# Identity products moved ahead of a conditioning step on TensorE, in a hand-ordered block of attention and a gated mixer

## The chip, the cores and the metric

The kernel runs on one core of one Trainium2 chip. The metric is device time in microseconds (us) of one execution, as the median of several. An execution is a little longer than the span of the instructions in its profile. Each core has TensorE (PE, matrix products), VectorE (DVE), ScalarE (ACT), GpSimd (POOL) and SyncE (SP, which here only issues transfers); they run on their own and wait for one another by semaphores.

## What is computed

The reference is a transformer block whose two branches are modulated by a conditioning vector c. All data are bf16, x has 2048 rows of 448.

```python
mod = (silu(c) @ w_mod).reshape(1, 6, 1, -1)          # sa, ca, ga, sb, cb, gb
h = layernorm(x) * (1 + ca) + sa
x = x + ga * A(h)      # 16 heads of 28, causal, window 256: softmax(q k^T) v, then wo
h = layernorm(x) * (1 + cb) + sb
x = x + gb * B(h)      # z = gelu(h w_in); z1 * (w_sp @ layernorm(z2) + b_sp), then w_out
```

What matters here is the beginning: sa and ca must be known, two pairs of x tiles (128 rows each) must be normalised, transposed and modulated, and only then can the first q and k be projected.

## The kernel before, in words

The whole program is a list of numbered operations, each made by a helper with its dependencies, and one hand-kept text, ORDER (lines 19 to 145), that says in which order each engine takes them. A word such as `57.p.2` means: operation 57 goes to TensorE (p; a is ACT, v is DVE, g is POOL, s is SP) and takes option 2 of what it has to hold, here a PSUM bank. `order` reads the words, `count` and `waits` work out the semaphores, and `emit` writes each engine's stream. An engine takes its stream strictly in that order, so an operation that waits holds up all that stand behind it on the same engine. A TensorE operation that only follows another TensorE operation into the same bank needs no semaphore.

The head of the program, up to about 20 us, works in these steps, each named by the line that the profile shows:

- Operation 46 (L518) turns the row c into a column; ScalarE takes the SiLU (L522, L523).
- Operations 54, 55 and 56 (created at L546, products at L540 with one at L544) form sa and ca from three pieces of w_mod: nine, sixteen and eight products with one column each. Each of the three waits for its own piece of wmod to land. VectorE copies the result to modT (L552, L553).
- Tiles 0 and 1 of x go through statistics (L605 to L617) and a norm (L625 on DVE, L627 on ACT). Operations 165 and 162 (L692) transpose them on TensorE, four products of 128 columns each; DVE (L701) and ACT (L699) apply sa and ca on the way into hT.
- WQK, the padded q and k weights, is copied together from wq_st by DVE and ACT (L596) and POOL (L597).
- Operations 174 to 183 (L740) project q for those 256 rows, first by slices of the contraction (174 and 175 use slice 0, 176 and 177 slice 1, 178 and 179 slice 2, two products each), then the last slice for each group; 188 to 191 begin k. qT and KT are copied out by L767 and L768.
- Tiles 2 and 3 follow the same path: statistics on DVE, the power on POOL (L613), the norms, then the transposes 168 and 171, the remaining projections, the exponentials (L913) on ScalarE, and attention proper.

Between these stand identity products, created by `warm` at lines 558 to 566 as operations 57 to 110: one product of the 128 x 128 identity with itself repeated over 512 columns (L561). Their result is never read. Of the 54, ORDER names those that are used, and the others are dropped. Each takes a PSUM bank from the list bA, whose options 0 to 7 are banks 6, 7, 0, 1, 2, 3, 4, 5. After the head the kernel runs attention tile by tile, then the gated mixer's first products (L1081, L1127), then the spatial mixing (L1151) and the output (L1170).

Of the kernel before, what the change touches and what calls it, by code (L numbers as in the profile page):

```python
# [17 lines left out]

ORDER = """
2.a 25.v 35.g 0.s 26.v 27.v 28.v 38.g 39.g 3.a 4.s 36.g 45.a 33.g 29.v 5.s 30.v 31.v 37.g 32.v 40.g 6.s 7.s 41.g 46.p.0 48.a 47.a 144.v 8.s 145.v 1.s  # L20
138.v 146.g 57.p.2 58.p.3 59.p.4 60.p.5 61.p.6 62.p.7 54.p.1 9.s 147.g 139.v 140.v 10.s 141.g 148.v 55.p 149.a.0 34.g 11.s 142.v 56.p 143.v.1 132.g
14.s 71.p.0 72.p.3 165.p.2 112.v 111.v 162.p.3 12.s 131.v 130.a 166.v 133.g 163.v 16.s 167.a 73.p.6 74.p.7 75.p.0 76.p.6 174.p.4.5 150.v 164.a 13.s
175.p.6.7 50.a 77.p.0 176.p 151.v 15.s 156.v 177.p 152.g 178.p 153.g 179.p 135.a 157.v 183.p 181.p 158.v 134.v 180.p 159.g 154.v 187.a 188.p.0.1 185.v
189.p.2.3 155.a.2 136.g 190.p 160.v 191.p 161.v.3 42.g 168.p.7 171.p.5 137.g 192.p 169.v 193.p 49.g 194.p 172.v 182.p 170.a 197.p 195.p 196.p 173.v
198.a 43.g 234.v 199.a 204.p.7 51.g 184.a 232.v 203.p.5 200.a 186.a 205.p.0 235.v 201.a 236.v 52.g 207.a 202.p.1 208.a 230.v 382.p.0 209.a 224.p.6
206.a 231.v 237.v 383.a.0 233.v 219.s 238.v 239.g 210.p.7 221.s 225.v 222.p.0 220.s 44.g 240.v 213.p.1 244.v.0 218.s 241.v.1 223.a 242.v.2 388.p.0
# [1228 lines left out]
```

## Time and profile before

| what | value |
|---|---|
| median of 3 runs | 273.93 us (273.01 to 274.91) |
| profiled execution | 275.39 us, span 273.7 us |
| TensorE busy | 266.2 us of the span |
| identity products (L561) | 13 in the span: 6, then 2, 4 and 1 |
| VectorE, ScalarE, POOL busy | 155.6, 137.9, 106.2 us |

A row of the profile's timeline gives the start and the length in us, the engine, the line of the kernel, the operation, the tile written and the tiles read, the shape, and the count of merged instructions; in brackets stands how long the engine was idle before and what ended that. A row of the chain of waits gives the start, the length and what the end of the program was waiting for then. Products on TensorE overlap, so the length of a merged row is the spacing times the count less one, and the duration of the last.

### The profile page before, as it was taken

To read this page: it belongs to the slowest core of one execution; us is meant where nothing else is said; L and a number is where in the kernel's file an instruction comes from. 1 tells how busy PE (TensorE), PEld (TensorE's weight loads), DVE (VectorE), ACT (ScalarE), POOL (GpSimd) and SP (SyncE) were. 2 spreads that over 40 slices of the span, in tenths; PEclk is the share of its full clock that TensorE was granted. 3 is DMA by queue.
4 is the path that set the end of the run, shared out by engine and by line. 5 is a ranking of instruction groups with operands and counts; after the bars stand their busy time and mean duration, and the time that the engine had idled before them with its cause. 6 is when DMAs were issued, how large, how long until landed. Compare 5 with 4: busy or idle time off the path is not lost.

```text
span 273.7 us, 7480 instructions
## 1 busy us (share of the span) xinstructions
PE 266.2 (97%) x3232; PEld 143.0 (52%) x3232; DVE 155.6 (57%) x380; ACT 137.9 (50%) x190; POOL 106.2 (39%) x161
## 2 busy tenths in 40 slices
PE   5989999999999999999999999999999999999995
PEld 2665565566578665545444444444444444444543
DVE  6689998799998999998483001131102321136533
ACT  3579999999999999799997400000000000000000
POOL 7650507401225715663458600646003631156220
PEclk9999999999999999999999999999999999999999
DMA  7938734633036755645999999500000000001212
GB/s 217 308 149 258 230 82 101 92 70 38 17 74 111 109 98 104 146 103 99 188 174 190 182 188 194 82 0 0 0 2 0 0 0 2 0 0 40 88 59 84
DMA packets 67594, 26.53 MB, mean 97 GB/s; under 512 B 58021, under 2 KB 66474, under 8 KB 67562
## 3 DMA queue, kind: packets, MB, share of 16 engines
q1 hardware_dynamic: 67288, 25.61, 45.4%
q8 instruction: 25, 0.41, 0.6%
q10 hardware_dynamic: 274, 0.46, 0.5%
q14 instruction: 7, 0.06, 0.1%
HBM read 9.53 MB, written 1.84 MB: 42 GB/s over the span
## 4 chain that ended last, share of the span: by engine, by line
PE 89%; ACT 7%; DMA 2%; DVE 1%; issue 1%; SPq 0%; DVEq 0%
PE ps L1151 35%; PE ps L1081 8%; PE ps L1127 8%; PE ps L1170 8%; PE ps L782 6%; PE ps L995 6%; PE ps L952 4%; ACT PW L913 4%; PE ps L1019 4%; PE ps L824 3%; PE ps L961 2%; DMA wmod<-in_w_mod_dram 2%; PE ps L811 1%; PE ps L561 1%; PE ps L740 1%; ACT qT L767 1%
## 5 line engine op out<-in xcount | busy, mean ns | idle before, releaser
L913 ACT ACTIVATE PW<-ps 128x2048 bf16<-128x2048 f32 (+1 forms) x56 | 67.9, 1255 | 1.8 <-PE ps L952 0.7
L1155 DVE TENSOR_TENSOR tmpg<-ps,bsp_bc 128x512 bf16<-128x512 f32 x28 | 19.0, 689 | 85.6 <-PE ps L1151 74.0
L1158 POOL TENSOR_TENSOR z1T<-tmpg,z1T 128x512 bf16<-128x512 bf16 x28 | 31.9, 1151 | 75.3 <-DVE tmpg L1155 75.3
L1151 PE MATMUL ps<-wspB,z 128*128 128x512 bf16 x224 | 49.5, 379 | 0.0
L1151 PE MATMUL ps<-wspA,z 128*128 128x512 bf16 x224 | 49.0, 379 | 0.0
L968 DVE TENSOR_TENSOR PT<-PW,mask 128x1024 bf16<-128x1024 bf16 x56 | 36.6, 681 | 0.7 <-ACT PW L913 0.7
L1151 PEld LDWEIGHTS ps<-wspA,z 128*128 128x128 bf16 x224 | 21.9, 98 | 26.7 <-POOL z L1096 0.5
L1151 PEld LDWEIGHTS ps<-wspB,z 128*128 128x128 bf16 x224 | 21.9, 98 | 26.3
L613 POOL TENSOR_TENSOR rs_all<-ve_all,neghalf 128x1 f32<-128x1 f32 (+1 forms) x31 | 20.6, 674 | 35.1 <-DVE ve_all L610 33.8
L995 PE MATMUL ps<-Vaug,PT 128*128 128x32 bf16 x496 | 23.9, 177 | 0.0
L995 PEld LDWEIGHTS ps<-Vaug,PT 128*128 128x128 bf16 x496 | 21.9, 96 | 3.8 <-DVE o_sb L1011 0.6
L1170 PE MATMUL ps<-w_out_g,z1T 128*128 128x448 bf16 (+2 forms) x126 | 21.9, 332 | 0.0
L1081 PE MATMUL ps<-w_in,hT 64*128 64x448 bf16 x224 | 21.9, 349 | 0.0
L1127 PE MATMUL ps<-hT,w_in 64*128 64x512 bf16 x196 | 21.8, 376 | 0.0
L995 PE MATMUL ps<-Vaug,PW 128*128 128x32 bf16 x224 | 20.2, 176 | 0.0
L782 PE MATMUL ps<-hT,WQK 128*128 128x512 bf16 x80 | 20.1, 380 | 0.0
L605 DVE BATCH_NORM_STATS2 st_all<-x_sb 128x6 f32<-128x448 bf16 x32 | 18.9, 610 | 0.0
L995 PEld LDWEIGHTS ps<-Vaug,PW 128*128 128x128 bf16 x224 | 17.6, 96 | 2.2
L1170 PEld LDWEIGHTS ps<-w_out_g,z1T 128*128 128x128 bf16 x126 | 11.7, 98 | 10.0
L1135 ACT ACTIVATE z1T<-ps 128x512 bf16<-128x512 f32 x28 | 14.3, 609 | 4.5 <-PE ps L1127 4.5
L1081 PEld LDWEIGHTS ps<-w_in,hT 64*128 64x128 bf16 x224 | 10.7, 94 | 10.6 <-ACT PW L913 0.4
L952 PE MATMUL ps<-qT,KT 32*128 32x64 bf16 (+2 forms) x1008 | 15.3, 198 | 0.3 <-ACT PW L913 0.2
(122 smaller groups left out, 343.5 us busy)
## 6 DMA issues: line engine op xcount, KB each, us to landing
out_dram<-fin SPq DMA_DIRECT2D x15, 112.0 KB, 1.7
x_sb<-in_A_x_dram SPq DMA_DIRECT2D x3, 448.0 KB, 4.2
wmod<-in_w_mod_dram SPq DMA_DIRECT2D x1, 1344.0 KB, 8.2
w_in<-in_B_w_in_dram SPq DMA_DIRECT2D x1, 1344.0 KB, 9.5
QBD<-qT SPq DMA_DIRECT2D x16, 64.0 KB, 2.1
w_out_g<-in_B_w_out_dram SPq DMA_DIRECT2D x1, 784.0 KB, 6.3
bsp_bc<-in_B_b_sp_dram SPq DMA_DIRECT2D x1, 512.0 KB, 5.4
x_sb<-in_A_x_dram SPq DMA_DIRECT2D x2, 224.0 KB, 3.7
```

Source lines behind the costliest of these rows:

```text
L613: rs = pool(0.41 + 0.155 * len(tiles), lambda e: e.tensor_tensor(rs_all[:, slot, a:b], ve_all[:, slot, a:b], neghalf[:, 0:b - a], ALU.pow) ...
L782: m = pe(4 * MMS, [lambda e, h=h, g=g, kc=kc, tb=tb: e.matmul(ps[:, h.slot[0], :], lhsT=WQK[:, kc, 4 * g:4 * g + 4, :].rearrange("p a b -> ...
L913: ex = act(xdur, lambda e, out_ap=out_ap, in_ap=in_ap: e.activation(out_ap(), in_ap(), ACT.Exp, scale=SCALE), [s], v - 8.0 + u, takes, tab ...
L952: fm.append(lambda e, hm=hm, k=k, qi=qi, key=key, kn=kn, lo=lo, hi=hi, col=col, p0=p0, t=t, j=j: e.matmul(ps[p0:p0 + kn, hm.slot[t], k * 1 ...
L968: return dve(0.68, lambda e: e.tensor_tensor(cols(hp.slot[0] * 2048 + 1024 * k, [[256, 4], [128, 2], [1, 128]]), cols(at_w() + 128 + 192 * ...
L995: fns.append(lambda e, hp=hp, hO=hO, hi=hi, bi=bi, kb=kb, hd=hd, nb=nb, a=at[hi][bi], p_of=p_of: e.matmul(ps[:, hO.slot[0], 32 * hd:32 * h ...
L1081: return lambda e, kc, p0, start, stop: e.matmul(ps[:, hs[t % 2].slot[hf], 0:D], lhsT=hT[p0:p0 + 64, kc, t * 128:(t + 1) * 128], rhs=w_in[ ...
L1127: return lambda e, kc, p0, start, stop: e.matmul(ps[:, hs[b // 2].slot[b % 2], :], lhsT=w_in[p0:p0 + 64, kc, ft * 128:(ft + 1) * 128], rhs ...
L1151: m = pe(16 * MMS, [lambda e, h=h, si=si, ft=ft, tb=tb: e.matmul(ps[:, h.slot[0], :], lhsT=z2[:, si, ft * 128:(ft + 1) * 128], rhs=(wspA i ...
L1155: a = dve(0.7, lambda e, h=h, ht=ht, tb=tb: e.tensor_tensor(tmpg[:, ht.slot[0], :], ps[:, h.slot[0], :], bsp_bc[:, tb * 512:(tb + 1) * 512 ...
L1158: u = pool(1.16, lambda e, ht=ht, ft=ft, tb=tb: e.tensor_tensor(z1T[tb][:, ft, :], tmpg[:, ht.slot[0], :], z1T[tb][:, ft, :], ALU.mult), [ ...
L1170: return [lambda e, ft=ft: e.matmul(ps[:, h.slot[0], c0:c1], lhsT=z1T[t // 4][:, ft, (t % 4) * 128:(t % 4 + 1) * 128], rhs=w_out_g[:, ft, ...
```

## The change

ORDER alone is changed; no operation is made differently. On TensorE the identity products are placed anew. The numbers 57, 58 and so on only count them off; all are the same product.

| place in TensorE's order | before | after |
|---|---|---|
| between 46 (c) and 54 (first L540 products) | 6 | 9 |
| between 56 (last L540 products) and 165 (first transposes) | 2 | 0 |
| between 162 (transposes) and 174 (first q products) | 4 | 3 |
| between 175 and 176 (q, slices 0 and 1) | 1 | 0 |
| in all | 13 | 12 |

The three that are added in front write banks 0, 1 and 2, which the first three have written; the three behind the transposes write banks 6, 4 and 5. Every other word stands in the same order on its engine; the rest of the changed lines is where the text breaks.

```diff
-138.v 146.g 57.p.2 58.p.3 59.p.4 60.p.5 61.p.6 62.p.7 54.p.1 9.s 147.g 139.v 140.v 10.s 141.g 148.v 55.p 149.a.0 34.g 11.s 142.v 56.p 143.v.1 132.g
-14.s 71.p.0 72.p.3 165.p.2 112.v 111.v 162.p.3 12.s 131.v 130.a 166.v 133.g 163.v 16.s 167.a 73.p.6 74.p.7 75.p.0 76.p.6 174.p.4.5 150.v 164.a 13.s
-175.p.6.7 50.a 77.p.0 176.p 151.v 15.s 156.v 177.p 152.g 178.p 153.g 179.p 135.a 157.v 183.p 181.p 158.v 134.v 180.p 159.g 154.v 187.a 188.p.0.1 185.v
+138.v 146.g 57.p.2 58.p.3 59.p.4 60.p.5 61.p.6 62.p.7 63.p.2 64.p.3 65.p.4 54.p.1 9.s 147.g 139.v 140.v 10.s 141.g 148.v 55.p 149.a.0 34.g 11.s 142.v
+56.p 143.v.1 132.g 14.s 165.p.2 112.v 111.v 162.p.3 12.s 131.v 130.a 166.v 133.g 163.v 16.s 167.a 71.p.0 72.p.6 73.p.7 174.p.4.5 150.v 164.a 13.s
+175.p.6.7 50.a 176.p 151.v 15.s 156.v 177.p 152.g 178.p 153.g 179.p 135.a 157.v 183.p 181.p 158.v 134.v 180.p 159.g 154.v 187.a 188.p.0.1 185.v
```

## The prediction on record

> **What bounds the kernel now.** I read the page first: its span, the busy shares, the granted clock and the shares of the chain that ended last.
>
> ```profile
> span 273.7 us, 7480 instructions
> PE 266.2 (97%) x3232; PEld 143.0 (52%) x3232; DVE 155.6 (57%) x380; ACT 137.9 (50%) x190; POOL 106.2 (39%) x161
> PEclk9999999999999999999999999999999999999999
> PE 89%; ACT 7%; DMA 2%; DVE 1%; issue 1%; SPq 0%; DVEq 0%
> ```
>
> TensorE carries 89% of the chain. The change touches only the first 14 us, so the question is where that stretch is not TensorE's own necessary work. The chain of waits in order of time answers (start, us, what):
>
> ```profile
> 1.80 5.27 DMA wmod<-in_w_mod_dram
> ...
> 7.12 0.37 PE ps L540 x8
> 7.50 0.88 PE ps L561 x2
> ...
> 12.61 0.42 DVE qT L768
> ...
> 13.28 0.98 DVE xn L625
> ...
> 20.89 0.22 PE ps L926
> ```
>
> The head is a relay: a piece of wmod lands at 7.07, the last eight L540 products follow, then identity products (L561) that compute nothing, then transposes, projections, a VectorE copy of qT and VectorE's norm of the second pair of x tiles. Only from 20.89 does TensorE work with hardly a wait, so what the relay saves should arrive at the end. The timeline of TensorE shows the pieces that the change reorders (start, us, line, shape, count):
>
> ```profile
> 2.39 2.74 PE L561 MATMUL ps<-ident 128*128 128x512 bf16 x6
> ...
> 5.11 0.35 PE L540 MATMUL ps<-sc_sb,wmod 128*128 128x1 bf16 x8
> 6.47 1.02 PE L540 MATMUL ps<-sc_sb,wmod 128*128 128x1 bf16 x24 [1.01 <-DMA wmod<-in_w_mod_dram]
> 7.36 1.01 PE L561 MATMUL ps<-ident 128*128 128x512 bf16 x2
> 8.16 1.06 PE L692 MATMUL ps<-ident,xn 128*128 128x128 bf16 x8
> 9.02 1.81 PE L561 MATMUL ps<-ident 128*128 128x512 bf16 x4
> 10.66 0.60 PE L740 MATMUL ps<-hT,WQK 128*128 128x256 bf16 x4
> 11.10 0.38 PE L561 MATMUL ps<-ident 128*128 128x512 bf16 x1
> 11.32 2.24 PE L740 MATMUL ps<-hT,WQK 128*128 128x256 bf16 x19
> ...
> 14.31 0.62 PE L692 MATMUL ps<-ident,xn 128*128 128x128 bf16 x8 [0.75 <-DVE xn L625]
> ```
>
> Two rates are to be seen. The first six identity products start (2.74 - 0.63)/5 = 0.42 us apart, when the last takes 0.63 (the last of the six; the two at 7.36 fit the same: the transposes start 0.80 after them, so 0.40 each). The one at 11.10 is followed 0.22 later. L692 starts every (1.06 - 0.31)/7 = 0.107 at 8.16 and every (0.62 - 0.22)/7 = 0.057 at 14.31. The rate doubles between: the four at 9.02 still fill 1.64 us, the L740 products at 10.66 already follow each other by 0.109. The page's clock digits read 9 from the first slice, so they do not show this slow start; the spacings do. (0.63, 0.31 and 0.22 are durations of single products, the longest and the shortest of each line; the answers by source line below give least, median and greatest in ns.)
>
> ```profile
> L561 PE MATMUL ps<-ident x13: 379/634/634, 2.4 to 11.1; 128*128 128x512 bf16 x13
> ```
> ```profile
> L692 PE MATMUL ps<-ident,xn x16: 219/272/314, 8.2 to 14.7; 128*128 128x128 bf16 x16
> ```
> ```profile
> L740 PE MATMUL ps<-hT,WQK x23: 272/273/273, 10.7 to 13.3; 128*128 128x256 bf16 x23
> ```
>
> **The change part by part.** *Three more identity products in front.* They write banks 0 to 2, which only identity products have touched, so they add no wait. At the slow rate nine of them end at 2.39 + 9 x 0.42, about 6.2, instead of 4.9. Behind them on TensorE stand nine tiny products (0.27 us, so 6.47), the next sixteen (16 x 0.026 = 0.42, so 6.9), and the last eight, which cannot start before the landing at 7.07 (chain). Before, the sixteen also started at 6.47. The cover is 0.15 us before 7.07; at worst, with all transfers early, the run would end no later than about 7.1, where it ends now at 7.36. Cost: 0.
>
> *The two identity products between L540 and the transposes are gone.* The transposes start at 7.36 instead of 8.16: 0.80 earlier. Who waits for them is VectorE:
>
> ```profile
> 8.07 0.28 DVE L596 COPY WQK<-wq_st 128x448 bf16<-128x448 bf16 x1 [0.30 <-DMA wq_st<-in_A_wqkv_dram]
> 8.84 0.84 DVE L701 TENSOR_SCALAR hT<-ps,modT 128x256 bf16<-128x256 bf16 x2 [0.49 <-PE ps L692]
> ...
> 11.45 0.17 DVE L617 SCALAR_TENSOR_TENSOR ve_all<-mv_all,rs_all 128x1 f32<-128x1 f32 x1
> 12.61 0.42 DVE L768 CAST qT<-ps 128x256 bf16<-128x256 f32 x1 [0.99 <-PE ps L740]
> 12.95 0.29 DVE L617 SCALAR_TENSOR_TENSOR ve_all<-mv_all,rs_all 128x1 f32<-128x1 f32 x1
> 13.28 0.97 DVE L625 TENSOR_SCALAR xn<-x_sb,mv_all,rs_all 128x448 bf16<-128x448 bf16 x1
> ```
>
> It sat 0.49 before the first hT, with its copy of WQK (held by a transfer until 8.07) in front. That copy ends at 8.35 and is next to decide: hT starts at 8.35 instead of 8.84. So 0.49 of the 0.80 passes, and hT's two are done at 8.35 + 0.84 = 9.19, ScalarE's two, which follow the first of them, at 10.30 - 0.49 = 9.8.
>
> ```profile
> 9.28 1.02 ACT L699 ACTIVATE hT<-ps,modT 128x256 bf16<-128x256 bf16 x2 [0.64 <-DVE hT L701]
> ```
>
> From 8.84 to 11.62 VectorE is packed, so all of it, the statistics too, moves by 0.49, and POOL's power with it:
>
> ```profile
> 10.83 1.14 POOL L613 TENSOR_TENSOR rs_all<-ve_all,neghalf 128x1 f32<-128x1 f32 x2
> 11.92 0.56 POOL L597 COPY WQK<-wq_st 128x448 bf16<-128x448 bf16 x1
> ...
> 13.17 0.95 POOL L531 MEMSET QBD<- 128x1024 f32 x1
> ```
>
> The power ends at 11.97 - 0.49 = 11.48.
>
> *Four identity products before L740 become three, and the single one at 11.10 goes.* After the eight transposes (7.36 + 8 x 0.107 = 8.21 at the slow rate) three take TensorE to 8.21 + 3 x 0.42 = 9.48, at the fast rate to 7.36 + 8 x 0.057 + 3 x 0.22 = 8.5. The first L740 product needs hT (9.19, 9.25 with the 0.06 that a signal takes here), so it starts at 9.48 or 9.25 instead of 10.66.
>
> *The sum* then hangs on when the rate doubles, which the trace of before cannot show for another order. (a) Where it doubles at 10.6 as now: four L740 at twice 0.109 take TensorE to 10.35, the next two start at 10.35 and 10.57, and the tenth behind the four, which qT waits for (11.32 + 9 x 0.109 + 0.27 = 12.57 now), starts about 11.47 and is done at 11.74; VectorE's qT starts at 11.78 instead of 12.61, 0.83 earlier. (b) Where it doubles a few us sooner: L740 starts at 9.25, the fifth waits for ScalarE until 9.87, the tenth behind the four starts at 9.87 + 9 x 0.109 = 10.85 and is done at 11.12; qT starts at 11.16, and L617 behind it (0.34 later now) at 11.50, where the power of POOL, done at 11.48, decides next: 11.53 instead of 12.95, 1.42 earlier.
>
> The norm L625 behind it takes 0.97 now beside POOL's memset of QBD (13.17 to 14.12). Moved to 11.86 it runs beside POOL's copies instead. Uncontended it would take 0.40 (the same line's row at 6.23):
>
> ```profile
> 6.23 0.40 DVE L625 TENSOR_SCALAR xn<-x_sb,mv_all,rs_all 128x448 bf16<-128x448 bf16 x1
> ```
>
> I keep 0.97, since POOL is as busy there; the other end would add 0.57. So the transposes at 14.31 move by 0.83 (a) or 1.42 (b), at best by 1.42 + 0.57 = 2.0.
>
> Behind 14.31 everything is driven by them, except transfers:
>
> ```profile
> 7.09 0.37 SPq L407 DMA_DIRECT2D x_sb<-in_A_x_dram  x1
> 8.60 0.60 SPq L403 DMA_DIRECT2D wv<-in_A_wqkv_dram  x1
> ```
> ```profile
> x_sb<-in_A_x_dram SPq DMA_DIRECT2D x3, 448.0 KB, 4.2
> wv<-in_A_wqkv_dram SPq DMA_DIRECT2D x1, 56.0 KB, 5.8
> ```
> ```profile
> 15.84 1.14 DVE L605 BATCH_NORM_STATS2 st_all<-x_sb 128x6 f32<-128x448 bf16 x2
> ```
> ```profile
> 18.05 0.93 PE L824 MATMUL ps<-wv,hT 128*128 128x448 bf16 x4
> ```
>
> The x tiles land near 7.09 + 4.2 = 11.3 and are used at 15.84; wv lands at 8.60 + 5.8 = 14.4 and is used at 18.05. Both leave over 3 us, so a shift of 1.4 meets no transfer. No queue of SP or POOL is moved past.
>
> Which of (a) and (b)? The six products from 2.39 to 4.9 did not raise the rate by 10.3; the unbroken work from 7.36 raised it after some 3.2 us. Nine products are 3.8 us unbroken, longer than that 3.2. By these rows (b) is nearer, and I take it. [...]
>
> (b) gives 275.39 - 1.42 = 273.97 for the profiled execution (275.39 in all, 1.7 of it around the span). The median of the runs, 273.93, lies 1.46 under that execution; 1.42 off the median is 272.5. But the runs reach from 273.01 to 274.91, a spread like that between an early and a late doubling; where the lowest already had an early one, 273.0 is what (b) can give. I take 272.7, between them.
>
> **The rivals.** *A, the rate doubles no earlier than now:* 0.83, so 273.93 - 0.83 = 273.1. For it: one run of six products raised nothing. Against: nine are half as long again. [...] *B, hidden:* the earlier start is swallowed before 20.89, 273.9. For it: most of the head is waits on other engines. Against: after 14.31 no row of the chain is a transfer. *C, slower:* with seven identity products behind L540 cut to three, the stretch from 7.36 holds fewer dense products, and the doubling is missed at 10.6 and comes one round (some 3.2 us) later, near 14. Then the L740 products run at 0.218: the tenth behind the first four starts at 10.35 + 9 x 0.218 = 12.31, and the last of the nine behind it is through at 12.31 + 10 x 0.218 = 14.5, so the second transposes start 0.2 late: 274.1. It decides only if the front run fails too and the rate is still slow beyond 12.3; were it slow through the second L740 batch (25 x 0.109), 2.7 more. For it: the first six alone failed. Against: L740 products fill TensorE as the identity products did.
>
> **How the numbers follow.** My forecast (b) has 0.50, A 0.26, B 0.13, C 0.11. The range: the low end is (b) with the norm uncontended, 273.93 - 2.0 = 271.9; the high end takes in B and C at 274.1 and 0.2 more, 274.3, for C's sum goes by a row that it has doubled. It leaves out some 0.15: C's dear form, and what none of the cases names. About 1% (2.7 us) is what a measurement of this kernel can tell from no change; no case reaches it but C's dear form on one side and (b) with a further gain downstream on the other, so faster 0.04, same 0.93, slower 0.03.
>
> **What would show it.** Right: nine L561 from 2.39 with the last ones at 0.22 apart or L692 at 0.057 already at 7.4 (for A at 0.107); L692 at 7.36; first hT at 8.35; first L740 near 9.3; VectorE's qT near 11.2 (A: 11.8); second L692 near 12.9 (A: 13.5); the L926 products at 20.89 near 19.5. Wrong: L540's last eight start after 7.2; hT stays at 8.8; L740 spaced 0.213 beyond 11; or a transfer releases TensorE between 14 and 21.

## The result and the profile after

| | before | after |
|---|---|---|
| median of 13 runs each, us | 274.91 (272.70 to 277.81) | 273.47 (272.82 to 275.15) |
| ratio, 95% interval | | 0.9951 (0.9928 to 0.9975) |
| profiled execution, us | 275.39, span 273.7 | 273.0, span 271.3 |

The change made the kernel 1.44 us faster by the medians, half a per cent. The three runs known before the prediction (median 273.93) lay low: thirteen give 274.91. The lowest runs of the two kernels hardly differ (272.70 and 272.82); below 273.5 lie four of the 13 of before and eight of the 13 after. So the change makes the short execution more frequent, not shorter. The ratio leaves out some of the longest runs of before, which is why it can stand nearer to one than the medians do.

The page of the changed kernel, in the rows shown of before:

```profile
span 271.3 us, 7454 instructions
PE 262.8 (97%) x3207; PEld 142.2 (52%) x3231; DVE 154.9 (57%) x380; ACT 137.9 (51%) x190; POOL 105.6 (39%) x161
PEclk9999999999999999999999999999999999999999
PE 84%; ACT 9%; DVE 2%; DMA 2%; issue 2%; SPq 1%; DVEq 0%
```

The shares hardly tell the two apart, and the clock digits are the same. TensorE's timeline does (start, us, line, shape, count):

```profile
2.38 3.94 PE L561 MATMUL ps<-ident 128*128 128x512 bf16 x9
6.16 0.17 PE L544 MATMUL ps<-xn,ident 128*128 128x8 bf16 x1
6.19 0.94 PE L540 MATMUL ps<-sc_sb,wmod 128*128 128x1 bf16 x32
6.99 0.61 PE L692 MATMUL ps<-ident,xn 128*128 128x128 bf16 x8
7.43 0.81 PE L561 MATMUL ps<-ident 128*128 128x512 bf16 x3
8.68 2.98 PE L740 MATMUL ps<-hT,WQK 128*128 128x256 bf16 x23 [0.43 <-DVE hT L701]
11.92 0.62 PE L692 MATMUL ps<-ident,xn 128*128 128x128 bf16 x8 [0.26 <-DVE xn L625]
```

The first L692 takes 0.61 for eight (1.06 before), the three L561 take 0.81 (0.22 apart), and the 23 L740 take 2.98, with the wait between their batches in it. So in this execution the full rate stands before 7.0, where the kernel before reached it between 10.3 and 10.66. TensorE now waits for others, 0.43 for hT and 0.26 for xn; it waited 0.75 for xn before. VectorE's rows follow:

```profile
7.70 0.28 DVE L596 COPY WQK<-wq_st 128x448 bf16<-128x448 bf16 x1 [0.31 <-DMA wq_st<-in_A_wqkv_dram]
7.89 0.72 DVE L701 TENSOR_SCALAR hT<-ps,modT 128x256 bf16<-128x256 bf16 x2
...
10.71 0.42 DVE L768 CAST qT<-ps 128x256 bf16<-128x256 f32 x1 [0.15 <-PE ps L740]
11.05 0.38 DVE L617 SCALAR_TENSOR_TENSOR ve_all<-mv_all,rs_all 128x1 f32<-128x1 f32 x1
11.47 0.40 DVE L625 TENSOR_SCALAR xn<-x_sb,mv_all,rs_all 128x448 bf16<-128x448 bf16 x1
```

The wait for L740 before qT shrank from 0.99 to 0.15, and the norm L625 takes 0.40 instead of 0.97. The chain of waits of the changed kernel, in order of time:

```profile
3.05 4.63 DMA wq_st<-in_A_wqkv_dram
...
9.41 1.28 PE ps L740 x10
...
11.47 0.41 DVE xn L625
...
18.50 0.29 PE ps L926 x8
```

It begins with the transfer of wq_st, no longer with wmod, and no identity product is left in it. L926, at 20.89 before, stands at 18.50: 2.39 earlier, and the span is 2.4 shorter (273.7 against 271.3). Everything behind the head takes the same 252.8 us in both. It does so, within 0.1, in the ten profiles of the experiments too, so one row, the start of that L926, reads off what the head is worth in each profiled execution.

### The profile page after: what moved, and what is told of

Same layout as the page of the kernel before. It is cut to its first block, busy times and chain, and to the rows that moved or that the text cites. A ratio compares the mean times of both kernels' runs of the same rounds, so it can differ in the third digit from the quotient of the medians.

```text
span 271.3 us, 7454 instructions
## 1 busy us (share of the span) xinstructions
PE 262.8 (97%) x3207; PEld 142.2 (52%) x3231; DVE 154.9 (57%) x380; ACT 137.9 (51%) x190; POOL 105.6 (39%) x161
## 3 DMA queue, kind: packets, MB, share of 16 engines
HBM read 9.53 MB, written 1.84 MB: 42 GB/s over the span
## 4 chain that ended last, share of the span: by engine, by line
PE 84%; ACT 9%; DVE 2%; DMA 2%; issue 2%; SPq 1%; DVEq 0%
PE ps L1151 35%; PE ps L1081 8%; PE ps L1127 8%; PE ps L1170 8%; PE ps L782 5%; ACT PW L913 5%; PE ps L995 5%; PE ps L952 4%; PE ps L1019 4%; PE ps L824 3%; PE ps L961 2%; DMA wq_st<-in_A_wqkv_dram 2%; DVE hT L728 1%; PE ps L811 1%; ACT qT L767 1%
## 5 line engine op out<-in xcount | busy, mean ns | idle before, releaser
L1151 PE MATMUL ps<-wspB,z 128*128 128x512 bf16 x218 | 48.8, 379 | 0.3
L782 PE MATMUL ps<-hT,WQK 128*128 128x512 bf16 x67 | 17.3, 379 | 1.3 <-DVE PT L988 0.2
```

Source lines behind the costliest of these rows:

```text
L782: m = pe(4 * MMS, [lambda e, h=h, g=g, kc=kc, tb=tb: e.matmul(ps[:, h.slot[0], :], lhsT=WQK[:, kc, 4 * g:4 * g + 4, :].rearrange("p a b -> ...
L1151: m = pe(16 * MMS, [lambda e, h=h, si=si, ft=ft, tb=tb: e.matmul(ps[:, h.slot[0], :], lhsT=z2[:, si, ft * 128:(ft + 1) * 128], rhs=(wspA i ...
```

## The experiments

Two theories to begin with. **F:** the longer run in front makes TensorE's rate double earlier, and that is the gain. **R:** the gain is that identity products no longer stand in front of the transposes and of L740. The edits are to TensorE's words in ORDER (`...` stands for words or lines left out). The numbers of identity products are those at the four places in the table of the change, in its order. Each median is of 8 to 12 runs, beside runs of the kernel before on the same chip.

| run | identity products | median, us (range) | ratio to before (interval) |
|---|---|---|---|
| nine in front, rest as before | 9, 2, 4, 1 | 273.35 (273.12 to 274.39) | 0.9955 (0.9936 to 0.9973) |
| six in front, rest as after | 6, 0, 3, 0 | 274.27 (272.97 to 275.90) | 0.9958 (0.9930 to 0.9986) |
| none | 0 | 274.72 (274.31 to 275.41) | 0.9988 (0.9963 to 1.0013) |
| nine in front, none behind | 9, 0, 0, 0 | 274.16 (272.81 to 275.18) | 0.9975 (0.9952 to 0.9998) |
| the changed kernel again | 9, 0, 3, 0 | 273.43 (272.96 to 275.12) | 0.9951 (0.9927 to 0.9974) |
| 36 transposes for the nine | 0, 0, 3, 0 | 273.59 (272.76 to 275.14) | 0.9961 (0.9927 to 0.9994) |
| early start, nine | 3 + 9, 0, 3, 0 | 273.22 (272.84 to 273.55) | 0.9940 (0.9912 to 0.9968) |
| twelve in front | 12, 0, 3, 0 | 273.82 (273.30 to 274.31) | 0.9952 (0.9933 to 0.9972) |
| early start, eight | 3 + 8, 0, 3, 0 | 273.07 (272.85 to 273.58) | 0.9936 (0.9917 to 0.9956) |
| nine, none behind, again | 9, 0, 0, 0 | 274.36 (272.99 to 275.59) | 0.9997 (0.9963 to 1.0031) |

The kernel before had a median of 274.94 beside the first four rows, 275.22 beside the next four and 274.94 beside the last two.

**Each half alone.** First the front half, then the other half:

```diff
-... 62.p.7 54.p.1 ...
+... 62.p.7 63.p.2 64.p.3 65.p.4 54.p.1 ...
```

> Nine identity products in front of L540 as in the changed kernel, and the seven behind (2, 4, 1) left as before. Theory F (the longer front run doubles TensorE's rate earlier, and that is the gain): identity products at 0.22 behind cost little, so the first hT is still at about 8.2 and the second transposes near 12.5 in the profile; median 273.4 to 273.8, and no runs above 276. Theory R (the gain is that identity products no longer stand in front of the transposes and of L740): nothing was removed, so the median stays near that of before, 274.9.

```diff
-... 62.p.7 63.p.2 64.p.3 65.p.4 54.p.1 ...
+... 62.p.7 54.p.1 ...
```

(against the changed kernel)

> Six in front as before, and behind as in the changed kernel (0, 3, 0). Theory R: the whole gain, median 273.5. Theory F: where the rate doubles late, removal gives 0.83 at most, so 274.1 or more, and the runs keep spreading to 276 or above; in the profile L692 starts at 7.4 with a spacing of 0.107.

The front half alone is as fast as the whole change: 273.35 against 273.47, with its seven products still standing in the way. R falls as the main cause. The profile of the front half is of an execution of 273.96 in which the rate doubled late, among the transposes (TensorE's timeline):

```profile
2.54 4.02 PE L561 MATMUL ps<-ident 128*128 128x512 bf16 x9
7.28 1.01 PE L561 MATMUL ps<-ident 128*128 128x512 bf16 x2
8.09 0.85 PE L692 MATMUL ps<-ident,xn 128*128 128x128 bf16 x8
8.78 1.03 PE L561 MATMUL ps<-ident 128*128 128x512 bf16 x4
```

The two L561 at 7.28 are still 0.40 apart, the four at 8.78 take 0.22 each. So theory F's times for the profile were missed: the first hT came at 8.76 instead of about 8.2, the second L692 at 12.80 instead of about 12.5.

The other half alone gives 0.67 between the medians, about what A of my rivals gave it (0.83). The intervals of the two halves, 0.9936 to 0.9973 and 0.9930 to 0.9986, do not tell them apart; against R stands the front half, in which nothing was removed. In the profiled execution of the other half the rate was still slow at the first transposes, TensorE's timeline:

```profile
7.15 1.01 PE L692 MATMUL ps<-ident,xn 128*128 128x128 bf16 x8
7.96 1.49 PE L561 MATMUL ps<-ident 128*128 128x512 bf16 x3
9.24 3.09 PE L740 MATMUL ps<-hT,WQK 128*128 128x256 bf16 x23
13.49 0.62 PE L692 MATMUL ps<-ident,xn 128*128 128x128 bf16 x8 [1.17 <-DVE xn L625]
```

The first L692 takes 1.01 (slow), the second 0.62. In this profile the norm L625 fell beside POOL's work and took 1.52 instead of 0.40:

```profile
11.91 1.52 DVE L625 TENSOR_SCALAR xn<-x_sb,mv_all,rs_all 128x448 bf16<-128x448 bf16 x1
12.36 0.95 POOL L531 MEMSET QBD<- 128x1024 f32 x1
```

That is 1.12 of the 1.57 by which its L926 (20.07) stands behind that of the changed kernel (18.50). The two halves, 1.59 and 0.67 between the medians, do not add up to the whole, 1.44. Why is only argued: with the full rate a product in the way costs 0.22 instead of 0.42, and less where TensorE would wait for hT.

**None at all.** The nine in front and the three behind are taken out of ORDER.

> No identity product at all. Theory R: as fast as the changed kernel or faster, 273.4 or less. Theory F: the rate doubles only after the first L740 batches, from 13 on; the batches run at 0.218 a product, the second transposes start after 14 and the L740 behind them partly at the slow rate too: median 275.5 to 277.5, slower than before.

Both theories missed. R's 273.4 did not come, and F's 275.5 to 277.5 did not either: 274.72, not to be told from before (the interval holds 1). The profile shows why:

```profile
7.35 1.01 PE L692 MATMUL ps<-ident,xn 128*128 128x128 bf16 x8
9.05 5.06 PE L740 MATMUL ps<-hT,WQK 128*128 128x256 bf16 x23 [0.69 <-DVE hT L701]
13.93 0.63 PE L692 MATMUL ps<-ident,xn 128*128 128x128 bf16 x8
```

All 23 L740 run at the slow rate (5.06), but they start at 9.05 instead of 10.66, and the second transposes stand at 13.93, already at the full rate, against 14.31 before. I had put them after 14 with slow products behind. So in these two executions the thirteen products of the kernel before gave back by their own length in the way what they won by the rate.

**Nine in front, none behind.**

```diff
-... 167.a 71.p.0 72.p.6 73.p.7 174.p.4.5 ...
+... 167.a 174.p.4.5 ...
```

> Nine in front, none behind. Theory R: as the changed kernel, 273.4 or a little less, since the last three in the way are gone. Theory F: the same median, 273.4 to 273.7, as long as the wait for hT from about 7.5 to 8.7 does not let the rate fall; if it does in some runs, these stand 1 to 2 us above.

The median came 0.7 above the changed kernel, with the runs drawn out from 272.81 to 275.18. In five of twelve runs the mean granted clock is 0.992 to 0.994. The first profile is of an execution of 273.11 without such a clock, so the same kernel was run once more:

> [...] F3 (the three behind keep the rate): half the runs or so again lie above 274 at such a clock, and a profile of such a run shows the rate fall between 7 and 12. If the spread came from elsewhere (landings): no low clock, median 273.5.

Six of the ten runs had such a clock, and the profile is of one. Together 14 of the 22 runs lie above 274, and 11 have the low clock; of the 25 runs of the changed kernel four lie above 274, and one (275.15) has it. So R falls here too: fewer products in the way is slower. The low clock is not the whole spread, since the longest run of either set (275.18 and 275.59) shows the full one. Busy time by stretches (stretch, its length, busy us and count of PE, PEld, DVE, ACT and POOL, then the granted clock, DMA share, GB/s), and TensorE's timeline:

```profile
6.00:8.00 2.00, 1.84 (x42) 1.40 (x40) 0.79 (x4) 0.44 (x1) 0.58 (x2) 1.00 1.11 303
8.00:10.00 2.00, 0.81 (x7) 0.32 (x5) 1.59 (x5) 1.65 (x4) 0.74 (x2) 0.91 0.96 281
10.00:12.00 2.00, 2.00 (x10) 1.44 (x11) 1.26 (x6) 1.35 (x2) 1.66 (x4) 0.50 1.14 337
12.00:14.00 2.00, 1.72 (x11) 1.09 (x9) 1.57 (x3) 1.03 (x2) 2.00 (x5) 0.74 1.06 188
```

```profile
7.48 0.61 PE L692 MATMUL ps<-ident,xn 128*128 128x128 bf16 x8
9.26 4.45 PE L740 MATMUL ps<-hT,WQK 128*128 128x256 bf16 x23 [1.18 <-DVE hT L701]
14.02 0.62 PE L692 MATMUL ps<-ident,xn 128*128 128x128 bf16 x8 [0.30 <-DVE xn L625]
```

The rate was full for the transposes at 7.48 (0.61), and lost again: clock 0.50 from 10 to 12, and by the mean clock of the stretches beside it (0.91 and 0.74) from about 10 - 0.09 x 2 / 0.5 = 9.64 to 12 + 0.26 x 2 / 0.5 = 13.04. The 23 L740 took 4.45 instead of 2.98, and the gain of the front run was gone. The three products behind fill most of the 1.18 that TensorE otherwise waits for hT; this is what they are worth.

**Transposes in front.** In place of each identity product, four transposes of the identity:

```diff
-    warm(14, [], 0.44, 1)
+    for _ in range(9):
+        hT_ = Hold(bA)
+        hT_.until.append(pe(0.44, [lambda e, h=hT_, i=i: e.matmul(
+            pst(h, i * 128, i * 128 + 128), lhsT=ident[:], rhs=ident[:], is_transpose=True) for i in range(4)], [t_ident], 900.0, [hT_]))
+    warm(5, [], 0.44, 1)
```

> The changed kernel itself once more, beside the next three on the same chip: 273.4, most runs between 272.8 and 273.8.

> The nine identity products in front are replaced by 36 transposes of the identity, four for each, which take as long at the slow rate (4 x 0.107); all else as in the changed kernel. If any work raises the rate (F1): the same 273.4. [...]

```profile
2.42 3.97 PE L567 MATMUL ps<-ident 128*128 128x128 bf16 x36
...
7.05 0.61 PE L696 MATMUL ps<-ident,xn 128*128 128x128 bf16 x8
```

(the lines below the edit are four further on; L696 is L692 elsewhere). The changed kernel again gave 273.43, the transposes 273.59, and in their profile the rate is full at 7.05, with nothing but the transposes in front of L544. F1 holds: transposes raise the rate as the identity products do (eight L696 in 0.61 here, eight L692 in 0.61 with identity products in front).

In its second profile the changed kernel doubled its rate sooner than in the first:

```profile
2.38 3.41 PE L561 MATMUL ps<-ident 128*128 128x512 bf16 x9
5.63 0.17 PE L544 MATMUL ps<-xn,ident 128*128 128x8 bf16 x1
...
6.43 0.91 PE L540 MATMUL ps<-sc_sb,wmod 128*128 128x1 bf16 x24 [0.44 <-DMA wmod<-in_w_mod_dram]
```

The nine take 3.41 instead of 3.94. With starts 0.42 apart before the doubling and 0.22 after it, L544 at 5.63 puts it at about 5.0, which is an estimate.

**More, and sooner.**

```diff
-... 65.p.4 54.p.1 ...
+... 65.p.4 66.p.5 67.p.6 68.p.7 54.p.1 ...
```

> Twelve in front instead of nine. My step said that nine cost nothing since L540's last piece lands at 7.07 and they are through 0.15 before. Then three more have no cover: at the rate of 0.42, L540 ends 1.1 later, at 0.22 some 0.5 later, and the first hT with them less the 0.4 that VectorE's copy of WQK holds it anyway: median 273.5 to 274.2. If the doubling alone mattered and the cover were large: 273.2 or less.

By the medians twelve in front cost 0.39 against the changed kernel beside it (273.82 against 273.43), inside what was expected of no cover; the ratios (0.9952 and 0.9951) do not show it. In its profile L540 ends later and the first hT with it (8.51). Then the start was moved ahead:

```diff
-2.a 25.v ... 46.p.0 48.a ...
+2.a 1236.v 25.v ... 1237.p.2 1238.p.3 1239.p.4 46.p.0 48.a ...
...
+    early, _, _ = alloc("early", [128, 128], BF16)
...
+    t_early = dve(0.1, lambda e: e.memset(early[:], 1.0))
+    for _ in range(3):
+        hE = Hold(bA)
+        hE.until.append(pe(0.44, [lambda e, h=hE: e.matmul(
+            ps[:, h.slot[0], :].rearrange("p (a b) -> p a b", b=128), lhsT=early[:], rhs=early[:].unsqueeze(1).broadcast_to([128, 4, 128]),
+            start=True, stop=True)], [t_early], 900.0, [hE]))
```

> Three more identity-like products ahead of operation 46, on a tile of ones that VectorE writes first, so that TensorE works from about 1.0 instead of 2.4 (the delay of 46 by 0.2 is covered until 6.2). [...] If a run of 3.8 did all that can be had: 273.4, the same spread. Theory R: no change, 273.5.

(1236 is the write of the tile; 1237 to 1239 are its products with itself over 512 columns.) The eight runs lie between 272.84 and 273.55: none above 274, where the changed kernel beside them reached 275.12, so the same spread did not come. Its profile shows the price, operation 46 pushed back and L544 at 6.62. With one identity product fewer (`65.p.4` out):

> The early start (three products on the tile of ones ahead of operation 46) with eight identity products in front of L540 instead of nine, so that the delay of 0.4 that the early start put on L540 in its profile (6.62 against 6.2) is given back. Theory F: still doubled early in every run, and the head 0.2 to 0.4 sooner: median 272.8 to 273.1, no run above 273.8. If what is left is set by the landing of wq_st alone: 273.2 as with nine.

273.07, inside F's 272.8 to 273.1, ten runs from 272.85 to 273.58: the fastest version by its median, 0.40 below the changed kernel, though the intervals do not tell the two apart; with nine the early start was as steady. Its profile, of the longest of the ten runs, is again released by a transfer, VectorE's copy of WQK by wq_st:

```profile
8.16 0.28 DVE L597 COPY WQK<-wq_st 128x448 bf16<-128x448 bf16 x1 [0.31 <-DMA wq_st<-in_A_wqkv_dram]
```

## Why the prediction was right

The mechanism was (b), an earlier doubling of the rate whose saving reaches the end. The time, 272.7, lies 0.8 under the 273.47 measured, inside the range; the step that was off is the base. I took 273.93 from three runs as the median of before and 273.0 as a bound from the lowest of them, and the median of more runs was 274.91. That the 1.42 forecast for the head meets the 1.44 between the medians is luck in part: the profiled pair, for which the 1.42 was worked out, gave 2.39, and each median is over executions that doubled at different moments. The bound of 273.0 did better: the lowest runs of both kernels agree (272.70 and 272.82), as where an early doubling was there already. The prediction also held that a change under about 1% could not be told from none; thirteen runs of each told half a per cent (0.9928 to 0.9975).

- **Three more in front cost nothing:** right in the outcome, not in the cover. In the profile after, L540's 32 products follow L544 without a wait (6.19, 0.94), so the last piece of wmod had landed before its turn, and the front run itself was the limit, with no 0.15 to spare. What covered it there was the 0.31 that VectorE still waited for wq_st. In the changed kernel's second profile, where the rate doubled within the nine, L540 did wait 0.44 for wmod.
- **The first hT at 8.35:** it came at 7.89. The copy of WQK in front of it was released at 7.70 instead of 8.07, 0.37 by the transfer, which differs from run to run (8.09 in the changed kernel's second profile). Besides, hT starts 0.19 after the start of that copy, not after its whole 0.28.
- **L740 near 9.3, qT near 11.2, second L692 near 12.9:** 8.68, 10.71 and 11.92. The order is as forecast, with 0.46 from the earlier hT and 0.57 from the norm. I kept 0.97 for it; it took 0.40, my other end. Over all twelve profiles it took 0.40 in the eight in which it started before POOL's last copy of WQK ahead of the memset of QBD. In the other four (before, six in front, none, and nine and none behind again) it ended 0.12 or 0.13 after the end of that memset and took 0.78 to 1.52. No run moved POOL's work, so that this is what held it up is read from the rows, not tested. The 2.39 of the profiled pair exceeds 1.42 by about these two.
- **All of it reaches the end:** right, with 252.8 behind L926 in every profile. B (hidden) falls with it.
- **When the rate doubles:** right in kind. I gave 0.50 to the early doubling; the half with nine in front alone, at 273.35, is the proof. The reason that I gave, nine being longer than the 3.2 that raised it once, was too simple, since the moment varies though the order up to L540 is the same. In the second profile of the changed kernel it came at about 5.0, with nine in front and the rest as before only after 8.09. Two of the 25 runs of the changed kernel lie above 275. One (275.15) has the mean clock of 0.994 that goes with a lost rate; the other (275.12) has the full one, and why it was long stays open.
- **A (removal alone):** a real part, 0.67 for 0.83 by the medians, but not seen beside the early rate. **C (slower, the rate missed for a round):** did not happen to the change. That a missed rise comes one round of some 3.2 later was my estimate from a single stretch, and no run shows it: with six in front and three behind, the 23 L740 from 9.24 on took 3.09, only 0.11 above the 2.98 of the full rate, and without identity products the 23 from 9.05 on stayed slow for all their 5.06. C's cost, slow L740 products, is what nine and none behind ran into (4.45), by a drop of the rate rather than by a missed rise.

What stays open: neither the longest runs of before, near 277, nor the lowest were caught in a profile, so that they are the ones with the latest and the earliest doubling is argued alone.

## What to carry to other kernels

Filler on TensorE was worth its place here where TensorE would have waited anyway. Nine in front were through before the transfer in the changed kernel's second profile, where L540 still waited 0.44 for wmod; twelve moved L544 from 6.16 to 6.86 in the profiles and the first hT from 7.89 to 8.51. In the relay a product cost its spacing, 0.42 at the slow rate and 0.22 at the full one. Place the filler as one run, as early as an operand can be had (that it has to be unbroken was not tested), and keep a little of it in later waits: without the three behind, 11 of 22 runs had the low clock, with them one of 25. And take a base from more than three runs where the runs spread by more than the gain.

## What the runs showed of the hardware

- The order of products did not fix when TensorE's rate doubled. In the five profiles with nine identity products in front, begun between 2.38 and 2.54, it doubled at moments from about 5.0 to after 8.09, by the spacings. Begun at 1.1, in two kernels, the runs kept within 0.7 us of each other, against 2.3 in the changed kernel.
- The rate was lost in one profile behind a wait of 1.18 us, for about 3.40 us (9.64 to 13.04, an estimate from the clocks of 0.91, 0.50 and 0.74 in the stretches from 8 to 14); TensorE was busy for 1.84 of the 2 us before 8 and for 0.81 of the 2 us behind. Behind a wait of 0.89 at the same place in the other profile of that kernel it was not lost (23 L740 in 2.98).
- The profile's clock showed full speed from the start, 1.00 from 0 to 6.2 in six profiles, also where products stood twice as far apart (before, the first identity products 0.42 instead of 0.22; without identity products the L740 from 9.05 on about 0.21 instead of 0.11, at a clock of 1.00 from 6 to 14). Spacing was the surer reading in the first microseconds.
